# Gated mix of softmax attention and a spectral filter: x brought to SBUF by transposing transfers

## The chip, the cores and the metric

The kernel runs on one NeuronCore of a Trainium2 chip. A core has five engines that work side by side, each through its own queue of instructions in order: TensorE (PE in the profile; its weight loads are PEld), VectorE (DVE), ScalarE (ACT), GpSimd (POOL) and SyncE (SP), which here only issues DMA transfers. The metric is the device time of one execution in microseconds. Before the change it is 399.11 us, the median of three runs (398.98 to 399.29).

## The reference

x has 2048 tokens of 448 channels in bf16. The result mixes an attention over 16 heads of 28 channels with a filter in the two-dimensional Fourier domain, by a gate for each token:

```python
g = _sigmoid((x * gate_w).sum(-1, keepdims=True))
a = _A_ref(x, A_wqkv, A_wo)
b = _B_ref(x, B_w_r, B_w_i)
return g * a + (1 - g) * b

# _A_ref
qkv = (x @ wqkv).reshape(B, S, 3, H, Dh).transpose(2, 0, 3, 1, 4)
q, k, v = qkv[0], qkv[1], qkv[2]
p = _softmax(jnp.einsum("bhqd,bhkd->bhqk", q, k) * Dh ** -0.5, axis=-1)
o = jnp.einsum("bhqk,bhkd->bhqd", p, v)
return o.transpose(0, 2, 1, 3).reshape(B, S, D) @ wo

# _B_ref
X = jnp.fft.rfft2(x.astype(jnp.float32), axes=(-2, -1))
X = X * (w_r + 1j * w_i)
return jnp.fft.irfft2(X, s=(S, D), axes=(-2, -1)).astype(jnp.bfloat16)
```

## The kernel before

The whole kernel is planned ahead. Class `Kernel` registers every instruction as an operation with an engine, a duration, its dependencies and a due key; `Sched.run` lays these out in a list schedule, and `build` emits them in that order. `pin` keeps that order in the program, so what an engine's queue holds behind a waiting instruction waits too. The durations and latencies in the code are the planner's assumptions and not measurements.

Layout. Token 16p + t lies on partition p, in column group t. `xtok` holds x by token (128 x 16 x 450), `xT[b]` holds four of these groups (512 tokens, "block b") transposed, in four chunks of channels. A matmul contracts over the partitions, so all projections need x with channels on partitions. Before, the four chunks are 112 even or odd channels each (CO), because the spectral part wants even and odd channels, and halves, apart. A row of ones at the end of the fourth chunk (row 113) carries a constant into the padded weights `wpad`.

Prologue (`prologue`, L737). x comes in by plain transfers. Block 0 is transposed on TensorE by 16 matmuls against the identity (L694) and copied to `xT[0]` by ScalarE and VectorE (L835, L837). 15 matmuls on zeros ahead of that (L812) warm the clock of TensorE. Then k and q of the first group of four heads are projected for block 0 (`project`), squared (L858), and the squared norms added in; psA, psB, pvb and the two banks bg are the places in PSUM.

Attention (`attention`, L1230). 16 (group of heads, block of queries) pairs are worked through in `self.steps`. A step holds two or three units; a unit is one head, 128 keys and 512 queries. TensorE writes the scores of a step to psA (three units) or psB (two), ScalarE takes the exponential into a ring of 28 units (L1350), and PV matmuls (`pv`, bank pvb) read the ring. Some key tiles go another way: scores into bg, then VectorE and GpSimd build approximate exponentials by integer arithmetic (L1304, L1316). In the first pair all keys are needed one after another, so k and v of blocks 0 to 3 are made while the exponentials already run: `x_block` (L964) transposes blocks 1 to 3 on TensorE and copies them by VectorE (L982, L990, L993), `proj_fast` projects k, `w_block` and `v_block` make the weighted v (`vw`; its column of weights is cast by GpSimd, L1136). For blocks 2 and 3 half of the transposes use the bank pvb (XPV, L195).

GpSimd clears and fills the padded weights of the other groups (`padset` L772, `padcopy` L786), from a planned time of 26 us on.

Spectral part (`background`, L1590), planned from TA (38 us) to TB (347 us) beside the attention. `fwd(t)` multiplies the 128 tokens of column group t, taken from `xT`, by a table `Bd` of cosines and sines; `fwd2`, the loop over 16 frequency groups (tables `CS`, filters `Wg`) and `out_tile` follow. `X1` is at first the place of raw weights (`U`), later of the result of `fwd`.

Queues. SP issues nearly all DMA transfers, ScalarE a few at the start. Each DMA waits for the completion of the DMA eight before it.

Of the kernel before, what the change touches and what calls it, by code (L numbers as in the profile page):

```python
# [22 lines left out]
FN = 113  # L23
CO = (0, 224, 1, 225)
# [40 lines left out]
def fft_consts():  # L65
# [4 lines left out]
    for ch, d0 in enumerate(CO):  # L70
        th = 2 * np.pi * (d0 + 2 * np.arange(112))[:, None] * f / D
        Bd[:112, ch] = np.concatenate([np.cos(th), -np.sin(th)], axis=1)
# [117 lines left out]
HAND = 0.15  # L190
RGD = 0.25
X1, F1 = -4975.96, -4886.98
W0, Q1 = 6, 17.61
XB = -0.52
XPV = (2, 3)  # L195
# [10 lines left out]
KN, KO, PLEAD, DSP, DHOLD, RWAIT, WREL, XLEAD, QLEAD, WLEAD = 0, 7.07, 2.64, 0, 2.12, 1.74, 7.73, 4.48, 20, 5.76  # L206
# [342 lines left out]
class Kernel:  # L549
# [4 lines left out]
    TA, TB = 37.99, 347.34  # L554
# [182 lines left out]
    def prologue(self):  # L737
# [7 lines left out]
        self.d_x = []  # L745
        self.d_x.append([self.dma(self.xtok[:, 0:2, 0:D], self.x[:, 0:2, :], (), K0, dur=0.45, lat=3.2),
                         self.dma(self.xtok[:, 2:4, 0:D], self.x[:, 2:4, :], (), K0 + .5, eng="AQ", dur=0.5, lat=3.4)])

        def wsrc(off, a, n, par):
            w = self.wqkv  # L750
            return _AP(tensor=w.tensor, offset=w.offset + par * 3 * D + off + a,
                       ap=[[6 * D, 112], [224 * 3 * D, 2], [1, n]])
        self.wsrc = wsrc

        def wload(t, off, a, n, key, eng, lat=3.0, deps=()):
            r = []
            for par in range(2):
                if isinstance(t, int):
                    o = free_dims(self.U[0:112], [[112, 2], [1, 112]], t + 224 * par)
                else:  # L760
                    o = t[0:112, 2 * par:2 * par + 2, 0:n]
                r.append(self.dma(o, wsrc(off, a, n, par), deps, key + 0.1 * par, eng=eng, dur=0.6, lat=lat))
            return r
        self.wload = wload
        dk = wload(self.wraw0["k"], D, 0, 112, K0 + 1, "SP", lat=2.9)
        dq = wload(self.wraw0["q"], 0, 0, 112, K0 + 2, "AQ", lat=3.2)
        ms = {}
        ms["zero"] = self.pool(0.3, lambda: self.pin(nc.gpsimd.memset(self.zero[:], 0.0)), (), K0)
        ms["xt"] = self.pool(0.1, lambda: self.pin(nc.gpsimd.memset(self.xtok[:, :, D + 1:D + 2], 1.0)), (), K0 + 1)
        self.pad_ms = {}  # L770

        def padset(w, g, key):  # L772
            t = self.wpad[w, g]
            m1 = self.pool(0.5, lambda t=t: self.pin(nc.gpsimd.memset(t[:], 0.0)),
                           () if g == 0 else self.wready["k", 0], key, rel=26.0 if g else 0.0)
            o = 1 if w == "q" else 0
            m2 = self.pool(0.1, lambda t=t: self.pin(nc.gpsimd.memset(
                free_dims(t[96:113, 3, :], [[32, 4]], o), 1.0)), (m1,), key + 0.01)
            m3 = self.pool(0.1, lambda t=t: self.pin(nc.gpsimd.memset(
                free_dims(t[96:112, 3, :], [[32, 4]], o), 0.0)), (m2,), key + 0.02)  # L780
            self.pad_ms[w, g] = m3
# [4 lines left out]
        def padcopy(w, g, raw, deps, key, eng):  # L786
            t = self.wpad[w, g]
            e = nc.vector if eng == "DVE" else nc.gpsimd

            def f1():  # L790
                self.pin(e.tensor_copy(out=free_dims(t[0:112], [[P, 2], [32, 4], [1, DH]], 2), in_=raw(0)))

            def f2():
                self.pin(e.tensor_copy(out=free_dims(t[0:112], [[P, 2], [32, 4], [1, DH]], 2 + 2 * P), in_=raw(1)))
            d = 0.22 if eng == "DVE" else 0.38
            a = sc.op(eng, d, f1, [deps[0], self.pad_ms[w, g]], key, name="padw")
            b = sc.op(eng, d, f2, [deps[1], self.pad_ms[w, g]], key + 0.01, name="padw")
            a.lk = b.lk = True
            return [a, b]
        self.padcopy = padcopy  # L800

        def raw0(w):
            def r(part):
                return free_dims(self.U[0:112], [[112, 2], [DH, 4], [1, DH]], self.wraw0[w] + 224 * part)
            return r
# [5 lines left out]
        for i in range(15):  # L811
# [3 lines left out]
        itq, itk = Item(), Item()  # L815
        itq.late = itk.late = True
        homes = [lambda: self.psB[:, 0, :], lambda: self.pv[:], lambda: self.bgi(itq), lambda: self.bgi(itk)]
        trs, self.xev = [[] for _ in range(4)], {}
        for h in range(2):
            for c in range(4):  # L820
                n = 113 if c == 3 else 112
                for t in (2 * h, 2 * h + 1):
                    def f(c=c, t=t, n=n):
                        o = homes[c]().bitcast(BF16)[0:n, 128 * t:128 * t + 128]
                        self.tr(o, self.xtok[:, t, CO[c]:CO[c] + 2 * n - 1:2])
                    trs[c].append(self.pe(128, f, (self.d_x[0][h], self.d_cst, ms["xt"]), K0 + 10 + 4 * h + c, dur=0.1,
                                          acq=(itq, itk)[c - 2] if c > 1 and t == 0 else None))
        for c in range(4):
            n = 113 if c == 3 else 112
            eng = "ACT" if c in (0, 2) else "DVE"  # L830

            def fe(c=c, n=n, eng=eng):
                src = homes[c]().bitcast(BF16)[0:n, 0:512]
                if eng == "ACT":
                    self.pin(nc.scalar.copy(out=self.xT[0][0:n, c, :], in_=src))  # L835
                else:
                    self.pin(nc.vector.tensor_copy(out=self.xT[0][0:n, c, :], in_=src))  # L837
            self.xev[0, c] = sc.op(eng, 0.36 if eng == "DVE" else 0.55, fe, trs[c], K0 + 11 + c,
                                   free=(None, None, itq, itk)[c], name="xev")
        trs = trs[3]  # L840
        self.kev, self.qev = {}, {}
        self.xtr = [trs[-1]]
# [3 lines left out]
        def project(b, w, lo, hi, key, stop):  # L846
            ops = []
            for c in range(4):
                r = 113 if c == 3 else 112

                def f(c=c, r=r):
                    self.mm(b[:, lo:hi], self.wpad[w, 0][0:r, c, :], self.xT[0][0:r, c, lo:hi], c == 0, stop and c == 3)
                ops.append(self.pe(hi - lo, f, [self.xev[0, c]] + self.wready[w, 0][c // 2:c // 2 + 1] + ops[-1:], key + .1 * c))
            return ops[-1]

        def square(i, b, lo, hi, dep):
            def fs():
                self.pin(nc.scalar.activation(out=self.sq[:, 512 * i + lo:512 * i + hi], in_=b[:, lo:hi], func=ACT.Square, scale=SQ))  # L858
            return self.act(0.1 + (hi - lo) / 1100.0, fs, (dep, tl, self.xev[0, 0], self.xev[0, 2]), K0 + 30 + i)

        kq = self.k[0]
        p1k = project(self.psB[:, 1, :], "k", 0, 256, K0 + 20, True)
        p1q = project(self.psA[:, 1, :], "q", 0, 512, K0 + 21, True)
        p1l = project(self.pv, "k", 256, 512, K0 + 25, True)
        for i, b, lo, hi, p1 in ((0, self.psB[:, 1, :], 0, 256, p1k), (2, self.pv, 256, 512, p1l)):
            a = square(i, b, lo, hi, p1)

            def fk(b=b, lo=lo, hi=hi):
                self.pin(nc.vector.tensor_scalar(out=kq[:, lo:hi], in0=b[:, lo:hi], scalar1=sv, scalar2=None, op0=ALU.mult))
            e = self.dve(0.38, fk, (p1,), K0 + 48 + i)  # L870

            def fm(i=i, b=b, lo=lo, hi=hi):
                self.mm(b[:, 256 - lo:512 - lo], self.c("selk"), self.sq[:, 512 * i + lo:512 * i + hi], True, True)
# [3 lines left out]
            def fd(b=b, lo=lo, hi=hi):  # L877
                self.pin(nc.vector.tensor_tensor(out=kq[:, lo:hi], in0=b[:, 256 - lo:512 - lo], in1=kq[:, lo:hi], op=ALU.add))
            evs["k", lo] = self.dve(0.36, fd, (m, e), K0 + 50 + i)
            if i == 0:  # L880
                a = square(1, self.psA[:, 1, :], 0, 512, p1q)
                qb = [self.psA[:, 0, :], self.psA[:, 2, :]]
                p2 = [project(qb[0], "q", 0, 256, K0 + 22, False), project(qb[1], "q", 256, 512, K0 + 23, False)]
                for j, eng in ((0, "ACT"), (1, "DVE")):
                    x = 256 * j

                    def fq(j=j, x=x):
                        self.mm(qb[j][:, x:x + 256], self.c("selq"), self.sq[:, 512 + x:768 + x], False, True)
                    m = self.pe(256, fq, (a, p2[j]), K0 + 20.5 + .1 * j)

                    def fe(j=j, x=x, eng=eng):
                        o, b = self.q[0][:, x:x + 256], qb[j][:, x:x + 256]
# [4 lines left out]
                    evs["q", x] = sc.op(eng, 0.45, fe, (m,), K0 + 49)  # L897
# [7 lines left out]
    def weights(self):  # L905
# [3 lines left out]
        for par in range(2):  # L909
            src = _AP(tensor=self.gw.tensor, offset=self.gw.offset + par, ap=[[2, 112], [224, 2], [1, 1]])  # L910
            gs.append(self.dma(self.wv0[0:112, 2 * par:2 * par + 2, 112:113], src, (), K + 5 + .1 * par, dur=0.3, lat=8.0))
        self.wvd = {0: self.wload(self.wv0, 2 * D, 0, 112, -4988.5, "SP", lat=5.0) + gs}
        for b in range(1, 4):
            self.d_x.append(self.dma(self.xtok[:, 4 * b:4 * b + 4, 0:D], self.x[:, 4 * b:4 * b + 4, :], (self.d_x[b - 1],) if b > 1 else (),
# [901 lines left out]
```

## Time and profile before

| | us |
|---|---|
| median of three runs | 399.11 |
| the profiled execution: its time | 399.57 |
| its span, first to last instruction | 397.7 |
| busy in the span: PE / ACT / DVE / POOL | 380.7 / 379.9 / 307.9 / 304.6 |
| exponentials (L1350), 165 from psA and 165 from psB, mean ns of one | 1648 and 1222 |
| first exponential starts | 12.48 |
| last exponential starts | 387.71 |

Successive exponentials overlap in the records, so that their means add up to more than their distance. A busy PE is not PE at its peak, since matmuls are pipelined. The line numbers are those of the kernel before; L691 and L694 are the helpers through which every matmul and every TensorE transpose goes, L666 the one through which every DMA goes.

### The profile page before, as it was taken

How to read it: one execution, taken by the hardware profiler on the slowest of the kernel's cores; microseconds unless marked ns; L12 is line 12 of the kernel's file. 1: busy time of each engine (PE TensorE's matmuls, PEld its weight loads, DVE VectorE, ACT ScalarE, POOL GpSimd, SP SyncE). 2: the span in 40 equal slices, each digit the busy share in tenths (PEclk: the TensorE clock that was granted, in tenths of full speed). 3: DMA queues.
4: the chain of work that ended last, by engine and by line, in shares of the span. 5: the costliest groups of instructions: out<-in, count | busy, mean ns of one | idle time of the engine just before them, and what ended most of it. 6: DMA issues, size and time to landing. Idle time of an engine off the chain costs nothing.

```text
span 397.7 us, 14802 instructions
## 1 busy us (share of the span) xinstructions
PE 380.7 (96%) x6311; PEld 155.7 (39%) x6311; DVE 307.9 (77%) x581; ACT 379.9 (96%) x350; POOL 304.6 (77%) x264
## 2 busy tenths in 40 slices
PE   8999999999999999999999999999999999999995
PEld 6453443334343332323443333344333443433333
DVE  2656987888887997988779888877888768676882
ACT  3879999999999999999999999999999999999992
POOL 6037589788756879998999889898799998878510
PEclk9999999999999999999999999999999999999999
DMA  7600003111213111211121212112110213120111
GB/s 188 161 3 3 6 12 89 30 50 27 55 27 87 42 49 43 59 37 32 38 63 40 55 35 60 34 44 64 40 45 27 85 59 108 57 80 2 39 40 48
DMA packets 31190, 20.51 MB, mean 52 GB/s; under 512 B 16424, under 2 KB 29204, under 8 KB 31124
## 3 DMA queue, kind: packets, MB, share of 16 engines
q1 hardware_dynamic: 30084, 19.02, 18.8%
q8 instruction: 49, 0.80, 0.9%
q10 hardware_dynamic: 1040, 0.55, 0.5%
q14 instruction: 17, 0.14, 0.1%
HBM read 13.67 MB, written 1.97 MB: 39 GB/s over the span
## 4 chain that ended last, share of the span: by engine, by line
ACT 61%; PE 27%; issue 8%; DMA 1%; DVE 1%; POOL 0%; DVEq 0%; ACTq 0%; POOLq 0%
ACT ring L1350 60%; PE bg L691 10%; PE pvb L691 7%; PE psA L691 5%; PE psB L691 4%; DMA xtok<-in_A_x_dram 1%; PE bg L694 1%; DVE pd L1304 0%; POOL pd L1316 0%; ACT w L1132 0%; PE pvb L694 0%; DVE pd L1316 0%; DVE Ab L1585 0%; DVEq L1811 0%; ACT q L894 0%
## 5 line engine op out<-in xcount | busy, mean ns | idle before, releaser
L1350 ACT ACTIVATE ring<-psA 128x1536 bf16<-128x1536 f32 x165 | 271.9, 1648 | 0.3 <-PE psA L691 0.3
L1316 POOL TENSOR_SCALAR pd<-pd 128x2048 uint16<-128x2048 uint16 x129 | 242.5, 1897 | 36.8 <-DVE pd L1304 18.5
L1350 ACT ACTIVATE ring<-psB 128x1024 bf16<-128x1024 f32 x165 | 201.7, 1222 | 1.4 <-PE pvb L691 1.4
L1304 DVE TENSOR_SCALAR pd<-bg 128x512 uint16<-128x512 f32 x200 | 134.5, 687 | 32.9 <-PE bg L691 28.8
L691 PEld LDWEIGHTS <-k 32*128 32x128 bf16 x1024 | 45.3, 91 | 116.1 <-issue 108.9
L691 PE MATMUL pvb<-ring,vw 128*32 128x512 bf16 x824 | 76.8, 384 | 0.3 <-DVE pvs L1486 0.3
L691 PE MATMUL bg<-q,k 32*128 32x512 bf16 x200 | 74.0, 382 | 0.0
L691 PE MATMUL pvb<-pd,vd 128*32 128x512 bf16 x800 | 71.9, 383 | 0.5 <-DVE pvs L1486 0.4
L691 PE MATMUL psA<-q,k 32*128 32x512 bf16 x495 | 64.9, 381 | 7.9 <-ACT ring L1350 4.6
L691 PE MATMUL psB<-q,k 32*128 32x512 bf16 x329 | 65.5, 382 | 1.9 <-ACT ring L1350 1.4
L691 PEld LDWEIGHTS <-vw 128*32 128x32 bf16 x824 | 20.7, 95 | 29.6 <-issue 25.9
L691 PEld LDWEIGHTS <-vd 128*32 128x32 bf16 x800 | 20.2, 95 | 25.0 <-issue 20.6
L1501 POOL TENSOR_TENSOR q<-pvs,Rb 128x512 bf16<-128x512 f32 x15 | 19.1, 1274 | 8.0 <-PE pvb L691 6.3
L691 PEld LDWEIGHTS <-xT 112*32 112x32 bf16 x1280 | 20.7, 96 | 9.7 <-issue 7.5
L1698 DVE TENSOR_TENSOR t<-bg,Wg 128x450 bf16<-128x450 f32 x32 | 19.3, 623 | 5.6 <-PE bg L691 4.5
L691 PE MATMUL pvb<-zero 128*32 128x256 bf16 (+5 forms) x432 | 18.3, 259 | 0.0
L691 PE MATMUL bg<-xT,wpk 112*32 112x512 bf16 (+1 forms) x240 | 18.2, 383 | 0.0
L691 PEld LDWEIGHTS <-zero 128*32 128x32 bf16 (+1 forms) x487 | 13.2, 97 | 12.9 <-issue 8.8
L691 PE MATMUL bg<-xT,wpq 112*32 112x512 bf16 (+1 forms) x240 | 18.0, 383 | 0.0
L691 PE MATMUL bg<-wo,q 128*32 128x448 bf16 x232 | 17.4, 355 | 0.2 <-DVE q L1479 0.2
L1136 POOL CAST vw<-w 128x16 bf16<-128x16 f32 (+1 forms) x7 | 2.4, 349 | 18.3 <-ACT w L1132 18.3
L1316 DVE TENSOR_SCALAR pd<-pd 128x2048 uint16<-128x2048 uint16 x21 | 15.0, 728 | 0.2
(131 smaller groups left out, 377.1 us busy)
## 6 DMA issues: line engine op xcount, KB each, us to landing
Rb<-rsc SPq DMA_DIRECT2D x60, 64.0 KB
CS<-cCS SPq DMA_DIRECT2D x16, 192.0 KB
xtok<-Ab SPq DMA_DIRECT2D x16, 112.5 KB
V<-xtok SPq DMA_DIRECT2D x16, 112.5 KB
xtok<-in_A_x_dram SPq DMA_DIRECT2D x3, 448.0 KB
out_dram<-fin SPq DMA_DIRECT2D x12, 112.0 KB
Wg<-in_B_w_r_dram SPq DMA_DIRECT2D x32, 28.1 KB
Wg<-in_B_w_i_dram SPq DMA_DIRECT2D x32, 28.1 KB
```

What stands on the lines that cost most here:

```text
L691: self.pin(self.nc.tensor.matmul(out, lhsT=lhsT, rhs=rhs, start=start, stop=stop, **kw))
L694: self.pin(self.nc.tensor.transpose(out=out, in_=in_, identity=self.c("ident")[0:n, 0:n]))
L1136: self.pin(nc.gpsimd.tensor_copy(out=free_dims(self.vw[g][:], [[32, 16 * nb]], 4 * b0 * 128 + DH), in_=free_dims(self.w[g][:], [[1, 16 * n ...
L1304: self.pin(nc.vector.tensor_scalar(out=ys[:, s, :].bitcast(U16), in0=self.bgi(it), scalar1=127 * UNITS, scalar2=0.0, op0=ALU.add, op1=ALU. ...
L1316: self.pin(e.tensor_scalar(out=fl(pds), in0=fl(ys), scalar1=float(PHASE[f]), scalar2=1.0, op0=ALU.add, op1=ALU.mult))
L1350: self.pin(nc.scalar.activation(out=self.ring[:, u0:u0 + len(st), :], in_=slot[:, 0:len(st), :], func=ACT.Exp, scale=LN2 / UNITS))
L1501: e = self.pool(1.15, lambda: self.pin(nc.gpsimd.tensor_tensor(out=dst, in0=pvs[:], in1=self.Rb[:], op=ALU.mult)), ds, kk)
L1698: self.pin(nc.vector.tensor_tensor(out=out[:], in0=self.bgi(it)[:, 0:F2].rearrange("p (a f) -> p a f", a=2), in1=free_dims(Wg[:], [[F - 2 ...
```

## The change

x is loaded in transposed form. `xload` issues one transposing DMA for each column group t of a block, 128 tokens by 512 columns from DRAM into `xT[b]`; 512 columns are the 448 of the token and 64 of the next one, which nobody reads. The last column group of the last block is loaded in parts, since it would read past the end of x: 112 tokens of four chunks, 16 tokens of three, and 64 x 16 single elements. The chunks are now 128, 128, 128 and 64 contiguous channels (CK), and the row of ones is row 65 of the fourth chunk, set by a memset (`ones`) on VectorE for block 0 and on GpSimd for the others. The weights are loaded in the same chunks, in a piece of 384 and one of 64 channels each; raw k weights of the first group now go through ScalarE's queue. `x_block` and the transposes and copies of the prologue are gone.

The spectral part still needs even and odd channels apart. x is loaded a second time, plainly, into `xtok`, behind the transposing loads; 16 copies on VectorE sort its channels into `X1` (256 columns of even channels, 224 of them used and 32 set to zero by a memset on GpSimd, then the same for odd ones); `fwd(t)` begins with a transposing DMA from `X1` to one of the two `CS` tiles and reads its chunks (128, 96, 128 and 96 rows) there.

Besides, the prologue warms with 24 matmuls (NWARM) in place of 15; the first k goes to a bg bank and the two halves of q to psB and a bg bank, in place of psB and two banks of psA; the padded weights are planned from 11 us on (RP) in place of 26; the spectral part starts at TA = 50. XDL, XTL and XTI are the planner's latencies and issue time for transposing transfers.

```diff
-CO = (0, 224, 1, 225)
+CO = ((0, 128), (256, 96), (1, 128), (257, 96))
+CK = (128, 128, 128, 64)
...
+RP = 11.0
+NWARM = 24
-X1, F1 = -4975.96, -4886.98
+F1 = -4900.0
-XB = -0.52
-XPV = (2, 3)
+XDL, XTL, XTI, FXL, XKL = 3.4, 0.9, 0.5, 25.0, 20.0
...
-    TA, TB = 37.99, 347.34
+    TA, TB = 50, 347.34
...
-        self.d_x.append([self.dma(self.xtok[:, 0:2, 0:D], self.x[:, 0:2, :], (), K0, dur=0.45, lat=3.2),
-                         self.dma(self.xtok[:, 2:4, 0:D], self.x[:, 2:4, :], (), K0 + .5, eng="AQ", dur=0.5, lat=3.4)])
+        def xload(b, t, key, dur=XTI):
+            src = lambda p, w: _AP(tensor=self.x.tensor, offset=self.x.offset + D * (16 * p + 4 * b + t),
+                                   ap=[[16 * D, 16 if p else 112 if (b, t) == (3, 3) else P], [1, w]])
+            dst, o = self.xT[b], 128 * t
+            lat = (XDL if b == 0 else 4.0) + XTL * t
+
+            def tr(out, in_):
+                return sc.op("SP", dur, lambda: self.pin(nc.sync.dma_start_transpose(out, in_)), (), key, 0.0, lat=lat, name="dma")
+            if (b, t) != (3, 3):
+                return [tr(dst[:, :, o:o + P], src(0, 512))]
+            r = [tr(dst[:, :, o:o + 112], src(0, 512)), tr(dst[:, 0:3, o + 112:o + P], src(112, 384))]
+
+            def el():
+                with nc.allow_non_contiguous_dma(reason="sixteen tokens"):
+                    self.pin(nc.sync.dma_start(out=dst[0:64, 3, o + 112:o + P], in_=_AP(
+                        tensor=self.x.tensor, offset=self.x.offset + D * (16 * 112 + 15) + 384, ap=[[1, 64], [16 * D, 16]])))
+            r.append(sc.op("SP", 0.6, el, r[:1], key + .5, 0.0, lat=5.0, name="dma"))
+            return r
...
+        def ones(b, eng, key):
+            e = nc.vector if eng == "DVE" else nc.gpsimd
+            o = sc.op(eng, 0.2 if eng == "DVE" else 0.35, lambda: self.pin(e.memset(self.xT[b][64:65, 3, :], 1.0)),
+                      [d for t in range(4) for d in self.d_x[b, t]], key, name="ones")
...
+        bk, bq, bl = (lambda: self.bgi(itk)), (lambda: self.psA[:, 1, :]), (lambda: self.pv[:])
...
-                qb = [self.psA[:, 0, :], self.psA[:, 2, :]]
+                qb = [lambda: self.psB[:, 0, :], lambda: self.bgi(itq)]
...
+        for t in range(4):
+            self.d_x[1, t] = self.xload(1, t, -4990.0 + .1 * t)
         self.wvd = {0: self.wload(self.wv0, 2 * D, 0, 112, -4988.5, "SP", lat=5.0) + gs}
+        for b in range(2, 4):
+            for t in range(4):
+                self.d_x[b, t] = self.xload(b, t, -4988.0 + b + .1 * t)
         for b in range(1, 4):
+            self.xone[b] = self.ones(b, "POOL", -4600.0 + b)
+        self.d_xt = [self.dma(self.xtok[:, 4 * b:4 * b + 4, 0:D], self.x[:, 4 * b:4 * b + 4, :], (self.d_x[3, 3][0],),
+                              K + 20 + b, dur=0.45, lat=4.0, rel=XKL) for b in range(4)]
...
-                self.x_block(b, X1 if b == 1 else due - XLEAD - XB * (b - 2))
...
+        padz = self.pool(1.2, lambda: self.pin(nc.gpsimd.memset(free_dims(self.X1[:], [[256, 2 * NT], [1, 32]], 224), 0.0)), pads,
+                         t_a - FXL - 1.0)
+        xd, xp = [], []
+        for t in range(NT):
+            def fx(t=t):
+                self.pin(nc.vector.tensor_copy(out=free_dims(self.X1[:], [[256, 2], [1, 224]], 512 * t),
+                                               in_=free_dims(self.xtok[:], [[1, 2], [2, 224]], 450 * t)))
+            o = self.dve(0.5, fx, pads + [self.d_xt[t // 4]], t_a - FXL + .5 * t)
...
+            xTp = self.CSt[t % 2]
+            d = sc.op("SP", XTI, lambda: self.pin(nc.sync.dma_start_transpose(xTp[:, 0:4, :], self.X1[:, t, :])),
+                      [padz, xd[t]] + xp[t - 2:t - 1 if t > 1 else 0], k - 5.0, k - W, lat=XDL, name="dma")
             for c in range(4):
                 def f(c=c):
-                    o = 2 * FN * (c // 2)
-                    self.mm4(self.bgi(it)[:, o:o + 2 * FN], self.xT[t // 4][0:112, c, 128 * (t % 4):128 * (t % 4) + 128],
-                             self.Bd[0:112, c, :], c % 2 == 0, c % 2 == 1)
+                    o, n = 2 * FN * (c // 2), CO[c][1]
+                    self.mm4(self.bgi(it)[:, o:o + 2 * FN], xTp[0:n, c, :], self.Bd[0:n, c, :], c % 2 == 0, c % 2 == 1)
```

197 lines of the change are left out of this document (74 added, 123 removed).

## The prediction

> **What bounds the kernel now.** I read the table of stretches first, then the chain of waits of the first 31 us, then ScalarE's timeline, then the DMA view of the start. In every stretch between 40 and 360 us ScalarE is busy without a gap:
>
> ```profile
> 40.00:80.00 40.00, 38.49 (x624) 15.67 (x623) 34.48 (x71) 40.00 (x38) 31.30 (x25) 1.00 0.14 34
> ```
>
> (the fourth busy figure, 40.00 of 40.00 us, is ScalarE's). It works through 330 exponentials (L1350), a pair each 2.24 us. What another engine saves there changes nothing. The time is set by when this stream starts, by what interrupts it before 40 us, and by the 9 us after its last exponential (388.5 us). The first part is this chain (start, length, what):
>
> ```profile
> 1.18 4.31 DMA xtok<-in_A_x_dram
> ...
> 5.53 0.46 PE psB L694 x2
> 5.99 0.21 PE pvb L694 x2
> 6.21 0.43 PE bg L694 x4
> ...
> 8.46 0.45 PE bg L694 x8
> 8.91 0.27 PE psB L691
> 9.17 0.45 PE bg L694 x8
> ...
> 10.43 0.48 ACT q L894
> 10.91 0.04 issue
> 10.96 0.38 PE psA L691 x2
> ...
> 12.48 1.45 ACT ring L1350
> ```
>
> The reader sees block 0 of x land at 5.49 us, its TensorE transposes (L694) follow, those of block 1 stand on the chain twice (8.46, 9.17), and near its end a ScalarE evacuation of one bank of psA holds a matmul into another bank of it. The first exponential starts at 12.48 us. The second loss is in ScalarE's timeline:
>
> ```profile
> 23.80 1.58 ACT L1350 ACTIVATE ring<-psA 128x1536 bf16<-128x1536 f32 x1
> 26.34 0.18 ACT L1132 ACTIVATE w<-bg 128x16 f32<-128x16 bf16 x1 [0.96 <-PE bg L694]
> 27.91 1.02 ACT L1350 ACTIVATE ring<-psB 128x1024 bf16<-128x1024 f32 x1 [1.38 <-PE pvb L691]
> ```
>
> An exponential from psA gives way to the next after 1.33 us (12.48 to 13.83 is 1.35), so the twelfth could have started at 25.13; it starts at 27.91. It writes units 28 and 29 into a ring of 28, so it needs the first PV matmul, and that one needs the bank pvb, which the transposes of blocks 2 and 3 use (XPV) until their copy ends at 27.08. From 27.91 on nothing stops the stream. So the forecast reduces to one number: when does the twelfth exponential start?
>
> **What the change removes at the start.** The 16 transposes of block 0, their four copies and the wait between landing and projection (5.49 to 6.67: 1.2 us); block 1's two groups on the chain (0.9 us); the psA serialisation (10.43 to 11.34: 0.9 us), since the two halves of q now have psB and a bg bank. That is 3.0 of the 7.0 us from landing to first exponential. Added: the instruction order now puts the square of the second half of k (0.39 us, L858) ahead of the evacuation of q on ScalarE. 7.0 - 3.0 + 0.4 = 4.4; I take 4.5. The PE queue opens with 24 warm-up matmuls instead of 15; 15 took 3.38 us from 1.10, so 24 end at 1.10 + 24 x 0.225 = 6.5.
>
> **What a transposing load costs** is the unknown: no row of before has one. Let d be the time by which each load of 128 tokens x 512 columns (128 KB) puts off the next. From below: plain bytes. The view of the first 8 us,
>
> ```profile
> DMA packets 3042, 1.35 MB, mean 169 GB/s; under 512 B 1861, under 2 KB 3042, under 8 KB 3042
> ...
> q1 hardware_dynamic: 2146, 0.92, 48.9%
> q10 hardware_dynamic: 896, 0.44, 21.3%
> ```
>
> has slices of 300 to 360 GB/s when full, so d is at least 0.4 us. It can't be below that by any row. From above: the destination of one load is 128 channels x 4 chunks of 256 B, 512 pieces; in a stretch of small transfers (118.4 to 123 us: 690 packets, 36.1% of 16 engines for 4.6 us) a packet took 38.5 ns, and 512 x 38.5 / 16 = 1.23 us. In the view above a packet of 444 B on average took 70.2% x 16 x 8 us / 3042 = 29.5 ns, 0.066 ns a byte, as do the 38.5 ns of the other stretch with its 580 B. By the byte, 512 pieces of 256 B take 0.54 us. I take d = 0.7: near the price by the byte, and something for a write pattern that no row has. Issue on SP is no limit below d = 0.5: L666's plain ones took 0.34 to 0.48 us each. The order shows each DMA waiting for the one eight before it, as now.
>
> DMA begins to move bytes at 1.6 us; 0.85 MB at 300 GB/s would have ended at 4.4 and landed at 5.49, so 1.1 us lie on top. With 0.3 MB of weights and constants (1.0 us) block 0 lands at 3.7 + 4d = 6.5, as the warm-up ends. First exponential: 6.5 + 4.5 = 11.0 (at d = 1.23: 8.6 + 4.5 = 13.1, and 8.2 + 4d in general).
>
> **Blocks 1 to 3.** The projections of block 1 stand on PE right behind the first two score groups, those of block 2 ahead of the fourth and those of block 3 behind the eleventh. PE waits in order, and scores wait behind. Block 2 lands at 3.7 + 0.3 (the v weights) + 12d = 12.4 and is wanted some 2.5 us after the first exponential, 13.5: no stall. Block 3 (19 transfers, one of 1024 single elements) is wanted near 23.5, some 17 or 18 at d = 0.7. A small loss, 0.25 us, where 12 projections of block 2 stand between two score groups (x12 took 0.82 us).
>
> **The twelfth exponential.** On PE the first PV now follows the thirteenth score group and one 0.25 us group; with the score (0.39), the PV and the hand-over, 1.3 us after the exponential was due. 12.65 (27.91's due time 25.13 less 12.48) + 11.0 + 0.25 + 1.3 = 25.2. GpSimd gives nearly the same: its casts of w into vw (L1136) now stand behind the padding of all weights, moved from 26.7 to 37 us to 11 us and after. From about 8.7: 6 weight memsets (0.53) with small ones, 4.2; the memset of vw, 1.8; 12 copies of 0.37 us per 224 elements, now 336 and 112, 4.2; a memset of vd, 1.8; three memsets of ones 1.0; two casts 0.5: 22.2, and one wait, for the elements of block 3 (near 21) ahead of vd, puts it at 23.7. Then 0.8 us of VectorE for vw (0.16 + 0.61), and PV. So 25.4 instead of 27.91: 2.5 us.
>
> **What is added later.** 16 sorting copies on VectorE, 448 elements each: no such row; the padding copy of 224 elements took 0.21 and a bf16 multiply of 512 took 0.42, so 0.35 to 0.6, 6 to 10 us. VectorE is busy 16.63 of 27.5 us from 12.5 to 40, and block copies of 1.5 us x 3 go; they fit, though evacuations of k and v queue behind them. One memset on GpSimd (1024 elements, 0.9 from 1.81 for 2048). 4 plain loads of x on SP behind all others. 16 transposes SBUF to SBUF on SP, each double-buffered. By the order of the instructions 8 or more score groups, 9 us (1.12 each), lie between the matmul that frees a buffer and the one that needs it. A plain DMA such as the row sums took 4 us until its reader ran (47.02 to 51.13). From below such a transpose costs nothing. From above, an SP queue held by the broadcast of G (52.2 to 59 us) leaves 4 us at the tightest; I take 0. If that cover went, PE would wait inside its queue and each us late would cost up to 16 us. Sum: 12.48 to 11.0 gives 1.5, the ring 1.0, together 2.5. The profiled run, 399.57 us (span 397.7 and 1.9 around it), goes to 397.1; it lay 0.46 above the median of 399.11, so **396.6** for the median.
>
> **Rivals.** (1) Slower: transposing loads as dear as packets. The twelfth starts 14.2 us (12.65 + 0.25 + 1.3) behind the first, so the gain is 13.7 less the first's start, 8.2 + 4d, less the stall once block 2 is late, (4.0 + 12d) - (10.7 + 4d) = 8d - 6.7; together 12.2 - 12d, zero at d = 1.02. At 1.23 the loss is 2.6 (401.7), at 1.6 it is 7.0 (406.1), at 2.0 11.8 (410.9). For it: 61% of the packets of the start are under 512 B already, and the DMA shows full slices; against: time went by the byte. The Trainium skill, "VectorE: DVE Perf Modes", section "The three transpose paths", gives 1309 ns for a crossbar DMA transpose of 128x128 and 390 ns on TensorE; taken as d for the whole load it would mean, as an estimate, a loss of 3.5 us, and four times that per load some 50 us. The same skill, "Advanced Engine Details and Errata", section "X-Bar Transpose (TRN2)", calls such transfers as fast as plain ones, which is d = 0.4 and the forecast. No row here decides between the two pages; they are why I leave this rival a large chance. (2) No change: GpSimd's casts come 2.5 us later (elements of block 3 near 23.5), so the twelfth exponential stays at 27.9: 399.1. For it: one in-order queue holds both. (3) Slower: the SBUF transposes come late on PE. 1 us at 8 of the 16 is 8 us less the gain: 404.6. For: SP's queue is in order; against: 9 us of cover.
>
> **Chances.** Forecast 0.48; rival 1 0.28; rival 2 0.10; rival 3 0.10; some other late stall in a plan whose spectral part starts 12 us later (TA 38 to 50) 0.04. Of these, faster by over 0.2% (0.8 us, about what a measurement tells from no change) 0.48, within 0.10, slower 0.42. Likeliest own range 395.6 to 398.2 (d 0.4 to 0.8). Range with the rivals up to d = 1.6: 395.6 to 406.
>
> **What would show it.** First exponential near 11.0; block 2's projections not waiting for DMA; the twelfth exponential near 25.4 with PV ending the wait; ScalarE 40.00 of 40.00 from 40 us on. Wrong if PE waits on DMA xT in the first 25 us, if x's transfers run past 18 us, or if PE waits on CS between 55 and 150 us.

## The result, and the profile after

The changed kernel takes 424.92 us (median of four runs, 421.77 to 426.87) against 399.17 us before: a ratio of 1.064 (95% interval 1.056 to 1.072). Its four runs spread over 5.1 us, those of the kernel before over 0.3. Ratios in this document leave out executions of a slower kind, such as one of 411.71 us at a granted clock of 0.974 beside three of the same kernel at 404.14 to 404.84 us and 0.998 to 1.0. The profiled execution is the one of 421.77 us, with a span of 420.0 us. It is 22.2 us longer than the profiled execution before. The forecast was 396.6 us, and its range ended at 406.

The table of stretches shows that ScalarE, the engine that set the end before, now has gaps (two rows of eight; the fourth busy figure is ScalarE's):

```profile
40.00:80.00 40.00, 38.61 (x588) 14.46 (x586) 31.43 (x68) 38.40 (x37) 21.80 (x16) 0.97 0.10 21
...
120.00:160.00 40.00, 38.74 (x692) 16.43 (x690) 31.70 (x68) 36.81 (x33) 25.59 (x16) 1.00 0.24 53
```

Before, each of these rows had 40.00 of 40.00. So there are losses at the start and losses much later. ScalarE's timeline of the start (start, length, what, and in brackets what ended the idle time) tells how the first exponentials fare:

```profile
13.13 1.45 ACT L1326 ACTIVATE ring<-psA 128x1536 bf16<-128x1536 f32 x1 [1.04 <-PE psA L693]
...
20.68 1.02 ACT L1326 ACTIVATE ring<-psB 128x1024 bf16<-128x1024 f32 x1 [3.77 <-PE psB L693]
22.95 1.45 ACT L1326 ACTIVATE ring<-psA 128x1536 bf16<-128x1536 f32 x1 [1.25 <-PE psA L693]
...
38.60 1.02 ACT L1326 ACTIVATE ring<-psB 128x1024 bf16<-128x1024 f32 x1 [5.19 <-PE pvb L693]
```

The first exponential starts 0.65 us later than before (12.48), the fourth 4.6 us later (16.06), the twelfth 10.7 us later (27.91). What holds them is in the chain of waits of the first 45 us, which is no longer made of matmuls:

```profile
0.74 1.33 SPq L756
2.07 0.06 issue
2.13 1.24 SPq L756
...
21.70 1.90 SPq L756
...
23.64 1.22 SPq L756
...
29.58 5.17 DMA xT<-in_A_x_dram
...
34.79 2.01 PE bg L693 x49
```

L756 is the transposing load. SP is held 1.22 to 1.90 us by each of the 17, 1.26 in the median, and the next one follows some 0.04 us later (2.07 and the like); the plain loads on the same queue took 0.31 to 0.55 us before. The 17 instructions, with two plain loads between them, last until 24.9 us. TensorE's timeline shows who waits, here for block 2:

```profile
19.38 0.62 PE L693 MATMUL bg<-xT,wpk 128*32 128x512 bf16 x4 [3.83 <-DMA xT<-in_A_x_dram]
```

The DMA engines aren't full meanwhile: the DMA view of the first 8 us (queue, packets, MB, share of 16 engines) has

```profile
q1 hardware_dynamic: 2488, 0.60, 38.5%
q10 hardware_dynamic: 1104, 0.31, 20.2%
```

that is 59% busy, where the kernel before had 70%. The instruction seems to be the bound, and not the bytes.

The later gaps lie at 119 to 132, 216 to 225 and 279 to 297 us, where the v projections of the other three groups of heads stand. TensorE's timeline has, after and then before (there the first group's, which stands in one piece):

```profile
125.07 1.75 PE L693 MATMUL bg<-wvr,xT 128*32 128x112 bf16 x64
```

```profile
17.48 1.02 PE L691 MATMUL bg<-wv,xT 112*32 112x113 bf16 x64
```

Sixty-four of these short matmuls took 1.75 us after and 1.02 before. Their number is the same. In the row after, every fourth one has 64 rows of weights (the name of the row is that of its first form).

### The profile page after: what moved, and what is told of

It reads as the page before. It is cut to its first block, busy times and chain, and to the rows that moved or that the text cites. A ratio compares the mean times of both kernels' runs of the same rounds, so it can differ in the third digit from the quotient of the medians.

```text
span 420.0 us, 14677 instructions
## 1 busy us (share of the span) xinstructions
PE 393.6 (94%) x6212; PEld 155.3 (37%) x6212; DVE 304.1 (72%) x587; ACT 381.1 (91%) x348; POOL 306.6 (73%) x259
## 4 chain that ended last, share of the span: by engine, by line
ACT 42%; PE 37%; issue 9%; SPq 7%; DVE 3%; DMA 2%; DVEq 0%; ACTq 0%
ACT ring L1326 42%; PE bg L693 15%; PE pvb L693 11%; PE psA L693 6%; SPq L756 5%; PE psB L693 4%; DVE pd L1280 1%; SPq L668 1%; DMA xT<-in_A_x_dram 1%; DMA rs<-pvs 0%; PE bg L696 0%; DVE vw L1160 0%; DVE X L1617 0%; DVE ft L1613 0%; DVE vd L1171 0%
## 5 line engine op out<-in xcount | busy, mean ns | idle before, releaser
L1326 ACT ACTIVATE ring<-psA 128x1536 bf16<-128x1536 f32 x165 | 261.2, 1583 | 11.4 <-PE psA L693 9.5
L1326 ACT ACTIVATE ring<-psB 128x1024 bf16<-128x1024 f32 x165 | 191.1, 1158 | 10.1 <-PE pvb L693 5.2
L693 PEld LDWEIGHTS <-k 32*128 32x128 bf16 x1024 | 44.1, 91 | 119.2 <-issue 112.1
L693 PE MATMUL psB<-q,k 32*128 32x512 bf16 x329 | 67.1, 386 | 2.0 <-ACT ring L1326 1.5
L693 PE MATMUL bg<-xT,wpk 128*32 128x512 bf16 (+2 forms) x244 | 19.4, 396 | 6.9 <-DMA xT<-in_A_x_dram 6.8
L693 PEld LDWEIGHTS <-xT 128*32 128x32 bf16 (+1 forms) x1024 | 19.1, 94 | 16.3 <-issue 6.5
L693 PE MATMUL bg<-wvr,xT 128*32 128x112 bf16 (+1 forms) x768 | 23.1, 217 | 0.2
L693 PEld LDWEIGHTS <-CS 128*32 128x32 bf16 (+1 forms) x640 | 15.0, 96 | 13.3 <-issue 7.3
L693 PE MATMUL bg<-xT,wpq 128*32 128x512 bf16 (+2 forms) x244 | 19.5, 398 | 0.0
L1001 DVE TENSOR_SCALAR q<-bg,cst 128x512 bf16<-128x512 f32 x15 | 11.3, 750 | 9.4 <-PE bg L693 9.2
```

The costliest lines, as they stand in the source:

```text
L693: self.pin(self.nc.tensor.matmul(out, lhsT=lhsT, rhs=rhs, start=start, stop=stop, **kw))
L1001: self.pin(nc.vector.tensor_scalar(out=dst, in0=self.bgi(it), scalar1=self.sv, scalar2=None, op0=ALU.mult))
L1326: self.pin(nc.scalar.activation(out=self.ring[:, u0:u0 + len(st), :], in_=slot[:, 0:len(st), :], func=ACT.Exp, scale=LN2 / UNITS))
```

## The experiments

All times below are medians; the kernel before took 399.07 to 399.33 us beside them. Unless said otherwise, delays are starts of exponentials against those of the kernel before (a table of them follows the experiments).

**Shapes by themselves.** A kernel with nothing but transposing transfers of many shapes on SP, and sets of 64 short matmuls on TensorE:

```diff
+nc.sync.dma_start_transpose(d[:], src(rows, cols, st, r * D))
...
+nc.tensor.matmul(b[32 * s:32 * s + 32, 112 * t:112 * t + 112],
+                 lhsT=w[0:n, c, 128 * t + 32 * s:128 * t + 32 * s + 32],
+                 rhs=w[0:n, c, 0:112], start=c == 0, stop=c == 3, tile_position=(0, 32 * s))
```

> Computes nothing of the reference: it copies x to the output and then times shapes. Transposing transfers, three of each: 128x512, 128x256, 128x128, 64x512, 64x128, 16x128 from DRAM, then 512x512, 512x128, 1024x128, 256x256 (rows contiguous in DRAM), plain 128x512, and 128x512, 128x128 and 128x2048 from SBUF. Theory A (a fixed price for each instruction on SP's queue): SP is held 1.2 to 1.3 us by every one of them, also by 16x128 and by 512x512, and by 0.3 to 0.6 us by the plain ones. Theory B (SP is held by the number of pieces that it writes out): 128x128 takes a quarter of 128x512, 0.3 us, and 512x512 four times, 5 us. On TensorE, sets of 64 short matmuls with 32-column weights and 112 moving columns: theory C (weights of 64 rows are dear, or the change between 64 and 128 rows is): rows 128,128,128,64 cost 1.6 to 1.8 us a set, and 128, 112 and 128,128,128,65 cost 0.9 to 1.0. Theory D (128 rows cost more than 112): 128 costs 1.6 or more, 112 costs 0.9. If 64 rows alone cost 0.9 and the mix 1.6, it is the change of rows.

The view by tile gives for each destination the least, the median and the longest hold of SP in ns (r16c128s is 16 tokens x 128 columns, sbt is 128x512 from SBUF, plain an ordinary 128x512 load):

```profile
L26 SPq DMA_TRANSPOSE r16c128s<-in_A_x_dram x3: 1222/1723/2137, 24.5 to 27.9; - x3
L26 SPq DMA_TRANSPOSE r1024c128s<-in_A_x_dram x3: 1306/1307/2197, 42.8 to 46.4; - x3
L26 SPq DMA_TRANSPOSE r512c512s<-in_A_x_dram x3: 1946/2396/3778, 29.7 to 34.1; - x3
L40 SPq DMA_DIRECT2D plain<-in_A_x_dram x3: 430/430/577, 52.0 to 53.1; - x3
L45 SPq DMA_TRANSPOSE sbt<-sb x3: 1195/1264/1265, 53.7 to 56.2; - x3
```

From 4 KB to 256 KB the least hold lies between 1.20 and 1.31 us, in the shapes not shown too: a price for each instruction, theory A. (Single holds were longer, up to 2.53 us; what held them isn't shown.) Only the two transfers of 512 KB take longer, 1.95 us at least for 512x512 and 1.92 for 128x2048 from SBUF, for four times the bytes of a 128x512 one. There theory A's 1.2 to 1.3 failed, and theory B's 5 us as well. On TensorE, in the order of the code (rows 112; then 128,128,128,64; then 128,128,128,65):

```profile
25.48 0.97 PE L74 MATMUL ps_k<-w 112*32 112x112 bf16 x64
...
30.86 1.75 PE L74 MATMUL ps_k128x3k<-w 128*32 128x112 bf16 x64
...
33.95 0.99 PE L74 MATMUL ps_k128x3k<-w 128*32 128x112 bf16 x64
```

Sets of 128, of 64 and of 65 rows alone took 0.97 us too (the second set of 64 rows 1.06, the second of 128,128,128,65 1.12). So neither 128 rows nor 64 rows are dear; the change between them is. A set has seven changes inside it, so one costs (1.75 - 0.97) / 7, some 0.1 us. The Trainium skill has a reason in "TensorEngine Tiling (Array Packing)", section "Key Properties": "Changing tiling mode (not just tile) drains the TensorE". The trace agrees that a change costs time; that it is a drain, no row here shows. With 65 rows in place of 64 the price is gone.

**The 65th row.** The changed kernel with the fourth chunk of v one row longer; its weights are zero:

```diff
-                n = CK[c]
+                n = 65 if c == 3 else P
...
+        wz = [self.pool(0.1, lambda w=w: self.pin(nc.gpsimd.memset(w[64:65, 3, :], 0.0)), (), -4600.5) for w in (self.wv0, self.wvr)]
```

> The changed kernel, with the fourth chunk of the v projections 65 rows in place of 64; the added row of the weights is zero. Theory C (64-row weights make the v projections dear): 64 of these matmuls take 0.9 to 1.0 us instead of 1.6 to 1.8, ScalarE has no gaps at 119 to 132, 216 to 225 and 279 to 297 us, the delay against the kernel before grows by at most 1 us after the 71st exponential instead of 8.2, and the run takes 412 to 415 us instead of 421.8. Theory D (128 rows): no change, 421 to 423 us.

412.55 us (412.23 to 412.68), 12.4 less than the changed kernel's median, from one row of zeros. The set that took 1.75 us now reads:

```profile
121.45 0.99 PE L693 MATMUL bg<-wvr,xT 128*32 128x112 bf16 x64
```

From the 14th to the 81st exponential, and from the 91st on, the delay doesn't grow by more than 0.3 us; one step of 1.3 us between is left, a little more than the 1 us that was expected at most.

**The same fault put into the kernel before.**

```diff
-                n = 112
+                n = 64 if c == 3 else 112
```

> The kernel before, with the fourth chunk of the v projections cut from 112 rows to 64 (48 channels of v are left out, less work). Theory C: 16 v projections of 64 matmuls become dearer by 0.6 to 0.8 us each and the time rises by some 8 us, to 404 to 409. Theory D: no change or slightly faster, 398.5 to 399.5.

409.54 us: 10.2 us more, a little beyond the forecast of theory C, for less work. Forty of these matmuls in one piece take 1.13 us (at 105.62 us), and 0.68 in the kernel before (at 103.25). The two runs show the cause from both sides.

**One issue for each block.** On top of the 65-row kernel, the 18 instructions for x become four (a block holds other tokens, and the load of single elements is left out):

```diff
+                    if t == 0:
+                        self.pin(nc.sync.dma_start_transpose(dst[:], _AP(
+                            tensor=self.x.tensor, offset=self.x.offset + 512 * D * b - (64 if b == 3 else 0), ap=[[D, 512], [1, 512]])))
```

> The kernel of the 65-row v projections (412.55 us), with one transposing transfer of 512 tokens x 512 columns for each block in place of four or more; block b holds tokens 512b to 512b+511 in place of 16p+4b+t (block 3 shifted by 64 elements), so q, k, v and the attention's rows belong to other tokens. Bytes and pieces that are moved are the same, the instructions on SP are 4 in place of 18. Theory A (the price of issuing on SP sets the landing of the blocks): block 2 lands before 15 us, TensorE doesn't wait for it by more than 0.5 us, the fourteenth exponential is at most 2 us behind the kernel before instead of 10.5, and the run takes 402 to 405 us. Theory B (the DMA engines are slow with pieces of 256 B): block 2 lands at 18 to 20 us as now, and the run takes 410 to 413.

401.82 us, 10.7 less, as theory A had it (0.2 us below its range). SP's timeline ends with x at 11.9 us in place of 24.9, and TensorE waits for no block:

```profile
0.74 5.01 SPq L758 DMA_TRANSPOSE xT<-in_A_x_dram  x2
...
7.07 4.86 SPq L758 DMA_TRANSPOSE xT<-in_A_x_dram  x2
```

The pieces are the same: 10,997 packets, of them 10,272 under 512 B, in the first 16 us here, and 11,436 with 10,626 in the first 29 us of the changed kernel, at 182 and 102 GB/s. The order on TensorE is the same too. Of the waits of TensorE that are gone, 4.6 us were for block 2, before the single elements are issued, and 2.0 us for these elements.

**Plain loads of the same bytes.**

```diff
-                return sc.op("SP", dur, lambda: self.pin(nc.sync.dma_start_transpose(out, in_)), (), key, 0.0, lat=lat, name="dma")
+                i = _AP(tensor=self.x.tensor, offset=self.x.offset + D * (4 * b + t) - (64 if (b, t) == (3, 3) else 0),
+                        ap=[[16 * D, P], [128, out.shape[1]], [1, n]])
+                return sc.op("SP", dur, lambda: self.pin(nc.sync.dma_start(out=out, in_=i)), (), key, 0.0, lat=lat, name="dma")
```

> The kernel of the 65-row v projections, with every transposing load of x replaced by a plain one of the same bytes in the same pieces of 256 B (x is not transposed, so all of attention works on wrong numbers). Theory A: SP is held 0.35 to 0.6 us by each, all 17 are issued by 10 us, block 0 lands near 6, the first exponential starts near 11, no wait for x, the twelfth exponential by 27, and the run takes 397 to 401 us: the forecast's own case d = 0.4 to 0.5, plus 1 us of a longer tail. Theory B: 256-byte pieces keep block 2 until 15 us or later, 406 or more.

400.10 us: within the expected range, though behind the kernel before (ratio 1.0023, 1.0012 to 1.0034). It is the forecast's own case. SP was held 0.51 us by each load in the median; with the gaps the 17 took (5.67 + 4.97) / 17 = 0.63 us each, near the d = 0.7 of the forecast, and were issued by 12.6 us, not by 10. ScalarE's timeline reads:

```profile
11.30 1.45 ACT L1330 ACTIVATE ring<-psA 128x1536 bf16<-128x1536 f32 x1 [1.04 <-PE psA L693]
...
25.41 1.02 ACT L1330 ACTIVATE ring<-psB 128x1024 bf16<-128x1024 f32 x1 [1.20 <-PE pvb L693]
```

The forecast had 11.0 and 25.4. The 2.4 us that are won there are lost again later, below.

**Keeping the clock up.** In the changed kernel the clock granted to TensorE fell to 0.50 in the stretch 20 to 23 us, behind the wait for block 2. Matmuls on zeros fill the waits of the 65-row kernel:

```diff
+                if (w, g, c) == ("k", 0, 0) and b in (2, 3):
+                    for i in range(36 if b == 2 else 16):
+                        self.mm(self.bgi(it)[:, 0:256], self.zero[:, 0:P], self.zero[:], True, True)
```

> The kernel of the 65-row v projections, with 36 matmuls on zeros ahead of the projection of k of block 2 and 16 ahead of that of block 3, which TensorE works through while it waits for x (4.6 and 2.0 us there). Landing times don't change. If the low clock after the waits (0.50 at 20 to 23 and 35 to 38 us) costs time, the clock stays above 0.9 there, twelve projections take 0.82 us instead of 1.47, and the run gains 1 to 3 us: 409.5 to 411.5. If the clock is only a sign of the waits: 412 to 413.5.

413.00 us, no gain. TensorE's timeline shows why that doesn't settle the price of the clock:

```profile
21.13 0.83 PE L693 MATMUL bg<-xT,wpk 128*32 128x512 bf16 x12
...
27.54 1.05 PE L693 MATMUL bg<-wv,xT 128*32 128x113 bf16 x52 [1.91 <-DMA wv<-in_gate_w_dram]
```

The twelve projections took 0.83 us in place of 1.47, and the fifth exponential was 5.5 us late in place of 6.5. Then the v projection waited for the weights of the gate, a plain load behind the transposing ones on SP, which let it start at 27.73 us without the filling and at 27.54 with it. The us that the clock was worth went into the next late load. The second filling ran at a clock of 0.50 and took 3.5 us, more than the 2.0 that it was to fill; at the 14th exponential both kernels are alike (10.2 and 10.5 us late).

**Parts of the change alone, in the kernel before.** The banks of q, then the bank pvb kept free (XPV empty), then both, then the start of the spectral part, then sorts and SBUF transposes with it:

```diff
-                qb = [self.psA[:, 0, :], self.psA[:, 2, :]]
+                qb = [lambda: self.psB[:, 0, :], lambda: self.bgi(it2)]
```

> The kernel before, with one part of the change alone: the two halves of q go to psB and a bg bank in place of two banks of psA. If the wait of psA (10.43 to 11.34 us) was worth what the forecast took for it, the first exponential starts 0.6 to 1.0 us earlier (11.5 to 11.9) and the run takes 398.3 to 398.8 us. If the banks are wanted by the transposes of block 1, which now stand behind, it is 399.3 or more.

399.21 us, ratio 1.0003 (0.9994 to 1.0012): nothing. The first exponential starts at 12.17 us; other kernels with the unchanged start have it between 11.89 and 12.48, so these 0.3 us are no gain that can be told from chance.

```diff
-XPV = (2, 3)
+XPV = ()
```

> The kernel before, with XPV empty: the transposes of blocks 2 and 3 use the bg banks alone, so the bank pvb is free for the PV matmuls from the start, and in the order the first PV stands behind 8 score groups in place of 13. If the twelfth exponential (27.91 us) waits only for PV behind those transposes, it starts at 25.1 to 25.5 and the run takes 396.2 to 397 us. If the transposes then wait for the bg banks and hold the scores behind them, the gain is under 1 us: 398.3 or more.

Slower, ratio 1.0131 (1.0113 to 1.0148). ScalarE's timeline shows both halves of it:

```profile
24.77 1.17 ACT L1350 ACTIVATE ring<-psB 128x1024 bf16<-128x1024 f32 x1
28.08 1.45 ACT L1350 ACTIVATE ring<-psA 128x1536 bf16<-128x1536 f32 x1 [2.15 <-PE psA L691]
```

The twelfth exponential no longer waits: 24.77 in place of 27.91, so pvb was the cause. The thirteenth waits in its place. Its scores stand on TensorE behind a v projection, a PV that waits for VectorE, and block 3's transposes in bg (24.05 to 27.5 us). Some 4.6 us more are lost at later places of this plan (from 0.75 ahead at the thirteenth exponential to 3.85 behind at the last).

> The kernel before with both: q's halves in psB and a bg bank, and XPV empty. If the two losses are apart and the bank of q is worth nothing (as measured, 399.21 against 399.09), it takes what XPV empty alone takes, within 0.4 us: 396.2 to 397.2 if the ring's wait was caused by pvb.

Ratio 1.0124 (1.0106 to 1.0141). That the pair takes what XPV empty alone takes held; the figure did not.

```diff
-    TA, TB = 37.99, 347.34
+    TA, TB = 50, 347.34
```

> The kernel before, with the spectral part planned from 50 us on in place of 38 (one constant of the change). In the repaired variants of the changed kernel the exponentials lose 1.3 us between the 81st and the 91st, and the stretch behind the last exponential is 1.1 us longer. Theory P (the later start crams the plan): both losses appear here, 400.5 to 402 us. Rival: they come from the sorts, the transposes SBUF to SBUF or the 128 rows; 399.0 to 399.5 here.

Ratio 1.009 (1.006 to 1.012), so theory P is half right: the stretch behind the last exponential's start grows from 10.0 to 12.9 us (span 400.1 less 387.23), but there is no loss between the 81st and the 91st exponential.

```diff
+            xTp = self.CSt[t % 2]
+            d = sc.op("SP", XTI, lambda: self.pin(nc.sync.dma_start_transpose(xTp[:, 0:4, :], self.X1[:, t, :])),
+                      [padz, xd[t]] + xp[t - 2:t - 1 if t > 1 else 0], k - 5.0, k - W, lat=XDL, name="dma")
```

> The kernel before's way of loading x, with the spectral part of the changed kernel: TA = 50, 16 sorts on VectorE, 16 transposes SBUF to SBUF on SP. If sorts and transposes are hidden as forecast, it takes what TA = 50 alone takes, within 0.5 us, and TensorE never waits for CS. If SP's price of 1.2 us for each transpose delays the spectral matmuls, it is 2 us or more above that, with PE waiting for CS between 55 and 160 us.

418.87 us, and one wait of ScalarE of 14.1 us for PV, which ends at 92.4 us, is most of it. But neither expected outcome came: TensorE never waits for CS, and the transposes held SP 1.24 us in the median and 2.09 at most. SP's timeline and GpSimd's tell what came ahead of the transposes:

```profile
50.71 16.52 SPq L668 DMA_DIRECT2D fin<-in_A_wo_dram  x7
67.88 3.41 SPq L1629 DMA_TRANSPOSE CS<-X  x2
```

```profile
65.56 0.47 POOL L949 MEMSET fin<- 128x448 bf16 x1
```

A load of wo waits 13.6 us on SP until GpSimd has cleared its target, which there stands behind 14.9 us of work for the attention, and the transposes stand behind the load in SP's queue. By the timelines, the spectral work that comes bunched behind that crowds VectorE and TensorE, and PV comes behind it; no further run tested this. So in this plan the cover of the transposes was absent, and the run doesn't price the transposes themselves.

**The start of the spectral part, in the kernel with one issue for each block.**

```diff
-    TA, TB = 50, 347.34
+    TA, TB = 38, 347.34
```

> The kernel with one transposing transfer for each block (401.82 us; tokens in another order), with the spectral part planned from 38 us on in place of 50. If the start at 50 us causes the late losses, the 1.3 us between the 81st and the 91st exponential and the longer end go, and it takes 399 to 400.5 us. If the sorts and the SBUF transposes cause them, it stays at 401 to 403, or PE waits for CS.

398.45 us, 3.4 less, and 0.14% below the kernel before (ratio 0.9986, 0.9977 to 0.9995), a little beyond the expected range. The step between the 81st and the 91st exponential is gone, and so is the longer end (span 397.0 less 386.93: 10.1 us). Sorts and SBUF transposes are in it and cost nothing that shows.

**Transposing loads where there is cover.** Blocks 0 and 1 go through TensorE as before, blocks 2 and 3 by transposing transfers; 65 rows; planning constants set anew (two sets). Core of the change against the 65-row kernel:

```diff
-        for t in range(4):
-            self.d_x[0, t] = xload(0, t, K0 + t)
+        self.d_x0 = [self.dma(self.xtok[:, 0:2, 0:D], self.x[:, 0:2, :], (), K0, dur=0.45, lat=3.2),
+                     self.dma(self.xtok[:, 2:4, 0:D], self.x[:, 2:4, :], (), K0 + .5, eng="AQ", dur=0.5, lat=3.4)]
...
+                        self.tr(o, self.xtok[:, t, 128 * c:128 * c + CK[c]])
...
-        for t in range(4):
-            self.d_x[1, t] = self.xload(1, t, -4990.0 + .1 * t)
+        d_x1 = self.dma(self.xtok[:, 4:8, 0:D], self.x[:, 4:8, :], (), -4990.0, dur=0.45, lat=3.0)
```

> The changed kernel with 65-row v projections, but blocks 0 and 1 of x loaded plainly and transposed on TensorE as in the kernel before; only blocks 2 and 3 come by transposing transfers (9 instructions and the single elements). Planning constants are set anew. If SP's price is the only thing against transposing loads, block 2 lands before 13 us and block 3 before 21, the first exponential starts at 11.9 to 12.8, the twelfth 12.6 to 13 us behind it (15.4 before), nothing is lost later, and it takes 396 to 398 us. If the transfers are late, PE waits for DMA xT and it takes 400 or more; if the wait of the ring moves elsewhere as it did with XPV empty, 399 to 404.

> The same with another set of planning constants (the transposes of block 1 stand behind the first scores): the first exponential some 1 us earlier, 10.8 to 11.8, the twelfth at 23.8 to 25, the run 396 to 398 us; rivals as before.

397.18 us (ratio 0.9950, 0.9938 to 0.9963) and 397.05 us (0.9947, 0.9934 to 0.9961): faster than both kernels. ScalarE's timeline of the first set, then SP's:

```profile
12.83 1.45 ACT L1378 ACTIVATE ring<-psA 128x1536 bf16<-128x1536 f32 x1 [0.49 <-PE psA L693]
...
25.52 1.14 ACT L1378 ACTIVATE ring<-psB 128x1024 bf16<-128x1024 f32 x1
```

```profile
5.12 5.24 SPq L756 DMA_TRANSPOSE xT<-in_A_x_dram  x4
...
12.28 7.13 SPq L756 DMA_TRANSPOSE xT<-in_A_x_dram  x5
```

The price is as it was (with the gaps, 1.31 us each for the four and 1.43 for the five), but nobody waits for these loads: the twelfth exponential starts 12.7 us behind the first, without a wait, where the kernel before needed 15.4. The second set starts the first at 11.40 and the twelfth at 24.04 us, as expected. Since the constants of the plan were set anew as well, the 0.5% belong to the version and not to the loads alone.

Starts of exponentials in us, and in brackets the delay against the kernel before:

```
exponential      1             4             12            81             91             330
before           12.48         16.06         27.91         105.77         117.12         387.71
changed          13.13 (+0.7)  20.68 (+4.6)  38.60 (+10.7) 119.32 (+13.6) 134.11 (+17.0) 408.86 (+21.2)
65 rows          12.99 (+0.5)  21.30 (+5.2)  37.27 (+9.4)  116.19 (+10.4) 128.88 (+11.8) 399.31 (+11.6)
one issue        13.14 (+0.7)  16.79 (+0.7)  27.16 (-0.8)  105.08 (-0.7)  117.76 (+0.6)  388.19 (+0.5)
plain loads      11.30 (-1.2)  14.95 (-1.1)  25.41 (-2.5)  103.63 (-2.1)  116.10 (-1.0)  387.29 (-0.4)
one issue, TA 38 12.87 (+0.4)  16.51 (+0.5)  27.32 (-0.6)  105.10 (-0.7)  116.40 (-0.7)  386.93 (-0.8)
two blocks, 1st  12.83 (+0.4)  16.52 (+0.5)  25.52 (-2.4)  103.58 (-2.2)  114.86 (-2.3)  385.44 (-2.3)
two blocks, 2nd  11.40 (-1.1)  15.04 (-1.0)  24.04 (-3.9)  102.74 (-3.0)  114.04 (-3.1)  386.09 (-1.6)
```

## Why the prediction was wrong

By medians the 25.8 us fall into three parts: 12.4 for the change of rows in the v projections (424.92 to 412.55), 12.4 for the price of the transposing loads (412.55 to 400.10), and 1.0 for the rest, which is 2.4 won at the start and 3.4 lost in the plan (the 3.4 as measured in the kernel with one issue for each block). The first part is known to some 3 us only, since the changed kernel's runs spread: by the profiled executions it is 9.5 (421.77 to 412.23). Two of the three signs that the prediction named for being wrong came: TensorE waits for xT at 19.38 us, and the transfers of x run past 18 us.

**The step that failed first** is the sentence "Issue on SP is no limit below d = 0.5: L666's plain ones took 0.34 to 0.48 us each". It took the issue time of one kind of instruction from the rows of another (which are 0.31 to 0.55 us, taken one by one). A transposing one holds SP 1.26 us, so d was 1.30 and not 0.7; whether 512 small pieces cost the DMA engines 0.54 or 1.23 us, which the working spent its bounds on, didn't matter. That the rival's 1.23, the time of 512 packets, lies near 1.30 is chance: a transfer of 4 KB holds SP as long. With d = 1.30 the sums of the first rival hold up well at first: first exponential at 8.2 + 4d = 13.4 (13.13), wait for block 2 of 8d - 6.7 = 3.7 (3.83 on TensorE). They end at a loss of 12d - 12.2 = 3.4 us because they stop there. Block 3 was counted as in time (with 19 transfers; there are 18); it comes last of all on SP, its single elements were issued at 29.58 and landed at 34.75, and PV stands behind its projections, so the ring's gain became a loss. Between the fourth and the ninth exponential 3.5 us came on top, in which TensorE ran in part at a clock of 0.50 and the v projections were slow: 10.7 us at the twelfth exponential in all.

Of the two sentences of the Trainium skill that the prediction set against each other, the 1309 ns of "VectorE: DVE Perf Modes", section "The three transpose paths", for 128x128 lies near the time that one instruction holds SP, at the least 1.23 us for 128x128 and 1.28 for 128x512. "Advanced Engine Details and Errata", section "X-Bar Transpose (TRN2)", has such transfers as fast as regular ones. The runs don't agree for 128 KB instructions: they hold SP 1.26 against 0.43 us, and the 17 of the changed kernel were on SP until 24.9 us, plain ones in the same pieces until 12.6.

**The step that wasn't there** is the v projections. The change was read as four chunks in place of four, with the same number of matmuls, and the 64 rows of the last went uncosted. Runs from both sides show it at 10 to 12 us. Sixteen sets at 0.78 us more make 12.5; where TensorE is busy 381 of 398 us, nearly all of it is paid.

**"Some other late stall in a plan whose spectral part starts 12 us later"** got a chance of 0.04. It came: 3.4 us between TA = 50 and TA = 38 in the kernel with one issue for each block, with the rest equal. But TA alone doesn't decide it. The kernel before with TA = 50 loses only at its end. With TA = 38 and XPV empty it has much the same step as the changed kernel's repaired variants (12.48 us from the 81st to the 91st exponential in place of 11.35). And the two-block versions start the spectral part at 50 too and have neither the step (11.28 and 11.30 us) nor a longer end (10.2 and 10.0 us behind the last exponential's start). So the stall belongs to each plan as a whole, and what in a plan makes the step stays open.

**What held.** With plain loads the first exponential came at 11.30 (11.0) and the twelfth at 25.41 (25.4), with PV ending the wait. That the ring waited for pvb was right. That sorts and SBUF transposes are hidden was right for the changed kernel, where TensorE never waits for CS, and the cover that it named seems to be what mattered: in the run where a load of wo held SP, the spectral part came late and, by the timelines, crowded out PV. The 0.9 us for the banks of q weren't there. Rival 2, late casts on GpSimd, wasn't seen where loads were in time. With loads at 0.5 us, 65 rows and TA = 38 the parts would add up to 396.7 (400.10 less 3.4), near the forecast; that sum wasn't run.

## What to carry to other kernels

Price an instruction you have no row for by its place in the queue that issues it, not only by its bytes: one DMA that holds its queue 1.3 us, seventeen times, is 22 us, and everything behind it is as late. When chunks are cut anew, look at the shapes of every matmul that uses them, above all at row counts that fall to 64 beside 128; one row of zeros may be the cheapest repair. And move a dear but asynchronous step to where something covers it, here to the last two blocks, rather than ahead of the first result.

## What was not expected of the hardware

A transposing DMA held SP 1.20 to 1.31 us at the least, for 16x128 (4 KB) as for 1024x128 (256 KB), from DRAM and from SBUF; a plain one of 128 KB 0.43 us. Alternating between 128 and 64 rows of weights cost some 0.1 us for each change, while all-64, all-112 and all-128 sets ran alike (0.97 us for 64 matmuls). A wait of 3.8 us on TensorE was followed by 3 us at half the clock, in which twelve projections of 512 columns took 1.47 in place of 0.83 us.
